# Sixteen float32 attention units by pairs of heads, and weight decoding pinned among VectorE's work

## The chip, the cores and the metric

The kernel runs on one NeuronCore of a Trainium2 chip. TensorE multiplies matrices into PSUM, VectorE (DVE in the rows), ScalarE (ACT) and GpSimd (POOL) work elementwise, SyncE (SP) issues DMAs. The metric is the device time of one execution in microseconds: before, the median of three runs is 740.23 us (740.11 to 740.49).

## The reference

Sliding-window attention with four sink keys, followed by a two-layer feed-forward block whose activation is a clipped square:

```python
scores = scale * q @ k.T                     # B, H, S, D = 4, 8, 768, 64
keep = (pos[None] < n_sink) | ((rel >= 0) & (rel < window))      # 4 sinks, window 128
a = exp(where(keep, scores, -1e9) - max); a = a / (a.sum(-1) + 1e-9)
x = (a @ v) as [3072, 512]
h = x @ w_in                                 # 512 x 2048, stored as float64
g = where(h >= 1, h, where(h <= -1, 0, (h + 1)**2 / 4))
out = g @ w_out                              # 2048 x 512, stored as float64
```

## The kernel before

A *unit* is one head and half of its 768 positions: three tiles of 128 queries, each against the block of 128 keys before, the 4 sinks and its own block. There are 64 units, in eight chunks of eight; chunk 0 is the first half of batch 0, chunk 1 the first half of batch 1, and so on. After a chunk of attention, the feed-forward block runs over its 384 rows, in 16 steps j of `stage1` (x times w_in, 12 products into `h_ps`) and `stage2` (g times w_out, 9 products into `o_ps`).

The first `NATIVE` = 12 units multiply in float32 directly. The other 52 are *split* units: each operand is written as a rounded float32r part and the rest, and each product is made of several fast ones. Feed-forward products are always split (3 for 1).

The weights come as float64 words in 16 loads of 1 MB (two j of w_in, then two j of w_out). `decode` rebuilds each as float32 parts: three integer passes on VectorE over 128 x 1024 elements (L151 to L153), a cast on ScalarE (L154) and a subtraction on VectorE (L155). `weights(n)` issues loads ahead, the first four from SyncE, the others from ScalarE's queue.

What sets the order: TensorE keeps the order of the program. `spread` interleaves two lists of steps by estimated TensorE weights: chunk 0's attention with the first `WFIRST` = 4 decodes, then the feed-forward steps of chunk 0, which carry the other 12 decodes, with the attention of chunk 1, and so on. On the other engines a scheduler places each instruction by its own estimate of when its inputs are there, so a decode may run far ahead of its place in the program.

A native unit before: `scores` (three products L244 over 128 partitions that hold q and k twice, hence the scale -0.0625; a masked scaling with the row's peak L248 on VectorE; the exponential with its sum L251 on ScalarE), the normalising of p (L256 on GpSimd, L257, L269 on ScalarE and L271 on VectorE), `transp` (seven transposes L324, L326 and three ScalarE copies) and `av` (four products L390 that leave 64 rows of x transposed, and a copy L392). `split` (L458, L459) then cuts x for the feed-forward block.

Of the kernel before, what the change touches and what calls it, by code (L numbers as in the profile page):

```python
# [51 lines left out]
def attn_ffn(ctx, tc, qk, vx, vs, par, w_in, w_out, out):  # L52
# [180 lines left out]
    def scores(u, i):  # L233
# [25 lines left out]
        c0 = 0  # L259
        if units.index(u) >= NATIVE:  # L260

            c0 = P
            nc.vector.tensor_tensor(p[:, i0:, KB:260], p[:, i0:, KB:260], p[:, i0:, 0:P], op=ALU.add)
        for i in range(CT):
            lo = KB if t0 + i == 0 else c0
            r = stat[:, CT + i:CT + i + 1]
            eng = NORM[i] if units.index(u) < NATIVE else "v"
            if eng == "a":
                nc.scalar.activation(p[:, i, lo:260], p[:, i, lo:260], AF.Copy, scale=r)  # L269
            else:  # L270
                (nc.gpsimd if eng == "p" else nc.vector).tensor_scalar(p[:, i, lo:260], p[:, i, lo:260], r, None,  # L271
                                                                       op0=ALU.mult)
        if units.index(u) < NATIVE:
            sk = None
        else:
            sk = att.tile([P, CT * NSINK], F32, name="sk")[:, :(CT - i0) * NSINK]
            nc.vector.tensor_copy(sk.rearrange("p (i s) -> p i s", s=NSINK), p[:, i0:, P:KB])
# [371 lines left out]
```

## Time and profile before

| | us |
|---|---|
| median of three runs | 740.23 |
| profiled execution, whole time | 741.25 |
| profiled execution, span from first to last instruction | 739.5 |
| TensorE busy | 703.0 (95%) |
| VectorE busy | 531.0 (72%) |
| ScalarE busy | 509.5 (69%) |
| GpSimd busy | 326.9 (44%) |

The shares are means over stages that differ: until the first feed-forward product TensorE has gaps, and after it nearly none. The profiled execution took 741.25 us, of which 1.75 us lie outside the span; it is 1.02 us longer than the median of the runs.

### The profile page before, as it was taken

How to read it: one execution, taken by the hardware profiler on the slowest of the kernel's cores; microseconds unless marked ns; L12 is line 12 of the kernel's file. 1: busy time of each engine (PE TensorE's matmuls, PEld its weight loads, DVE VectorE, ACT ScalarE, POOL GpSimd, SP SyncE). 2: the span in 40 equal slices, each digit the busy share in tenths (PEclk: the TensorE clock that was granted, in tenths of full speed). 3: DMA queues.
4: the chain of work that ended last, by engine and by line, in shares of the span. 5: the costliest groups of instructions: out<-in, count | busy, mean ns of one | idle time of the engine just before them, and what ended most of it. 6: DMA issues, size and time to landing. Idle time of an engine off the chain costs nothing.

```text
span 739.5 us, 12343 instructions
## 1 busy us (share of the span) xinstructions
PE 703.0 (95%) x3837; PEld 621.8 (84%) x3837; DVE 531.0 (72%) x1360; ACT 509.5 (69%) x1309; POOL 326.9 (44%) x562
## 2 busy tenths in 40 slices
PE   3787899999999999999999999999989999999996
PEld 2444788899999999999889998899979999989995
DVE  7999955757776887877877887878888577742221
ACT  4787676767777877777776876778767776544332
POOL 3111456754554454645565564646556344400000
PEclk9999999999999999999999999999999999999999
DMA  8977331213123433334434433424422220001001
GB/s 295 332 252 253 97 99 44 58 46 95 55 60 132 144 116 114 99 111 124 135 89 123 142 117 96 121 68 161 123 85 67 64 78 28 9 1 44 0 1 47
DMA packets 43236, 76.25 MB, mean 103 GB/s; under 512 B 7324, under 2 KB 27804, under 8 KB 43164
## 3 DMA queue, kind: packets, MB, share of 16 engines
q1 hardware_dynamic: 39900, 62.81, 27.5%
q10 hardware_dynamic: 3264, 12.58, 4.8%
q8 instruction: 32, 0.52, 0.3%
q14 instruction: 40, 0.33, 0.1%
HBM read 69.09 MB, written 6.29 MB: 102 GB/s over the span
## 4 chain that ended last, share of the span: by engine, by line
PE 72%; DVE 11%; ACT 6%; DMA 4%; issue 3%; POOL 2%; SPq 0%; ACTq 0%; POOLq 0%
PE h_ps L428 30%; PE o_ps L447 30%; PE ps_a L390 6%; PE ps_a L244 4%; ACT p L251 2%; PE ps_a L336 2%; DVE p L271 1%; DMA w<-w_in 1%; POOL stat L256 1%; DVE k_s L228 1%; DVE bits L152 1%; DMA again<-w_in 1%; DVE bits L153 1%; DMA r<-qk 1%; DVE g L437 1%
## 5 line engine op out<-in xcount | busy, mean ns | idle before, releaser
L428 PE MATMUL h_ps<-x,wi 128*128 128x384 f32 x1536 | 310.2, 341 | 2.8 <-DVE g L437 1.9
L428 PEld LDWEIGHTS h_ps<-x,wi 128*128 128x128 f32 x1536 | 263.6, 189 | 11.8 <-DVE g L437 2.2
L447 PE MATMUL o_ps<-w,gh 128*128 128x512 f32 x768 | 243.0, 397 | 0.0
L447 PE MATMUL o_ps<-w,gl 128*128 128x512 f32 x384 | 151.0, 393 | 0.0
L447 PEld LDWEIGHTS o_ps<-w,gh 128*128 128x128 f32 x768 | 134.0, 188 | 15.3 <-ACT g L436 0.4
L251 ACT ACTIVATE p<-p,peak 128x260 f32<-128x260 f32 (+1 forms) x192 | 93.9, 489 | 35.6 <-DVE peak L248 34.3
L435 ACT ACTIVATE g<-h_ps,half 128x384 f32<-128x384 f32 x128 | 74.0, 578 | 61.7 <-PE h_ps L428 61.2
L230 POOL TENSOR_TENSOR q_l<-r,q_h 128x384 fp32r<-128x384 f32 x52 | 53.8, 1034 | 137.9 <-ACT q_h L229 120.3
L437 DVE SCALAR_TENSOR_TENSOR g<-g,h_ps 128x384 f32<-128x384 f32 x128 | 70.2, 548 | 60.1 <-ACT g L436 59.2
L438 ACT CAST gh<-g 128x384 fp32r<-128x384 f32 x128 | 65.5, 512 | 52.8 <-DVE g L437 52.0
L248 DVE CUSTOM_DVE_ANT_0 p<-ps_a,m 128x260 f32<-128x260 f32 (+1 forms) x192 | 74.5, 400 | 24.8 <-PE ps_a L244 23.5
L447 PEld LDWEIGHTS o_ps<-w,gl 128*128 128x128 f32 x384 | 72.0, 188 | 17.3
L439 DVE TENSOR_TENSOR gl<-g,gh 128x384 fp32r<-128x384 f32 x112 | 68.2, 609 | 24.4 <-ACT gh L438 23.4
L228 DVE TENSOR_TENSOR k_s<-k_r,k_s 64x524 fp32r<-64x524 f32 (+1 forms) x46 | 48.1, 1047 | 43.6 <-ACT k_s L226 43.5
L244 PE MATMUL ps_a<-k_s,q_h 128*128 128x260 f32 (+1 forms) x228 | 65.9, 332 | 14.2 <-DMA k_s<-qk 7.6
L390 PE MATMUL ps_a<-pt,v_s 128*128 128x256 f32 (+2 forms) x396 | 68.2, 297 | 1.4 <-DVE peak L248 1.1
L436 ACT ACTIVATE g<-g 128x384 f32<-128x384 f32 x128 | 67.0, 524 | 2.6
L390 PEld LDWEIGHTS ps_a<-pt,v_s 128*128 128x128 f32 (+1 forms) x396 | 58.9, 183 | 9.5 <-issue 2.4
L244 PEld LDWEIGHTS ps_a<-k_s,q_h 128*128 128x128 f32 x228 | 43.2, 204 | 27.3 <-issue 8.5
L256 POOL TENSOR_SCALAR stat<-stat 128x3 f32<-128x3 f32 x64 | 32.7, 511 | 72.4 <-ACT p L251 60.6
L348 POOL TENSOR_SCALAR_AFFINE_SELECT pt<-pt 128x384 fp32r<-128x384 f32 (+1 forms) x104 | 53.8, 519 | 24.0 <-DVE pt L341 21.0
L271 DVE TENSOR_SCALAR p<-p,stat 128x132 f32<-128x132 f32 (+1 forms) x168 | 62.9, 424 | 0.2
(108 smaller groups left out, 954.5 us busy)
## 6 DMA issues: line engine op xcount, KB each, us to landing
r<-qk SPq DMA_DIRECT2D x52, 192.0 KB
k_r<-qk SPq DMA_DIRECT2D x32, 262.0 KB
again<-w_in SPq DMA_DIRECT2D x16, 512.0 KB
again<-w_out SPq DMA_DIRECT2D x16, 512.0 KB
w<-w_in ACTq DMA_DIRECT2D x6, 1024.0 KB
w<-w_out ACTq DMA_DIRECT2D x6, 1024.0 KB
out<-o SPq DMA_DIRECT2D x23, 256.0 KB
r<-vx SPq DMA_DIRECT2D x32, 128.0 KB
```

Source lines behind the costliest of these rows:

```text
L244: nc.tensor.matmul(ps[:, lo:260], lhsT=q[:, i * P:(i + 1) * P], rhs=k_s[:, c0:c0 + 260 - lo], start=(j == 0), stop=(j == len(qs) - 1))
L248: nc.vector.tensor_tensor_reduce(out=p[:, i, lo:260], in0=ps[:, lo:260], in1=m, scale=-0.0625 if units.index(u) < NATIVE else -0.125, scal ...
L251: nc.scalar.activation(p[:, i, lo:260], p[:, i, lo:260], AF.Exp, bias=peak_i, scale=-1.0, accum_out=stat[:, i:i + 1])
L271: (nc.gpsimd if eng == "p" else nc.vector).tensor_scalar(p[:, i, lo:260], p[:, i, lo:260], r, None, op0=ALU.mult)
L390: nc.tensor.matmul(z, lhsT=w, rhs=y, start=(n == 0), stop=(n == len(mms) - 1))
L428: nc.tensor.matmul(h_ps[:, :T], lhsT=w_i[j][:, w, ct * P:(ct + 1) * P], rhs=x[:, y, ct], start=(ct == 0 and n == 0), stop=(ct == NCT - 1 a ...
L435: nc.scalar.activation(g, h_ps[:, :T], AF.Relu, bias=half, scale=0.5)
L436: nc.scalar.activation(g, g, AF.Square)
L437: nc.vector.scalar_tensor_tensor(g, g, 1.0, h_ps[:, :T], op0=ALU.min, op1=ALU.max)
L438: nc.scalar.copy(gh, g)
L439: (nc.gpsimd if row0 == GL_POOL else nc.vector).tensor_tensor(gl, g, gh.bitcast(F32), op=ALU.subtract)
L447: nc.tensor.matmul(o_ps[tt], lhsT=gg[:, tt * P:(tt + 1) * P], rhs=w_o[j][:, w], start=(j == 0 and n == 0), stop=(j == NJ - 1 and n == 2))
```

## The change

Units 0 to 15 (chunks 0 and 1) are now native, in pairs of heads. One new input `qkp` holds a pair's two heads in the two halves of the 128 partitions, so each score product contracts over 64 partitions, and a pair needs one load of q and one of k. p is not normalised: it is transposed as it leaves the exponential, and becomes the stationary operand of products with v, to which a column of ones is added; column 65 of the result is the sum, and a VectorE pass divides the three tiles by it (`early_av`). Three transposes per pair (`pair_x`) bring x into the layout that `split` reads. In the tile of the first queries but one, a new mask `m1n` lets the sinks be read from the block before. Chunk 0's scores also use the PSUM tiles of the feed-forward block.

The first instruction of every decode is kept at its place in the program's order on VectorE, and the first four weight loads are issued after a pair's k load. Units 16 to 63 are computed as before; the subtraction of k in units 16 to 19 is on GpSimd (before: 12 to 17).

```diff
-NATIVE = 12
+NATIVE = 16
-KL_POOL = range(12, 18)
+KL_POOL = range(16, 20)
...
+    m1n = const.tile([P, 260], F32, name="m1n")
...
+    nc.vector.tensor_copy(m1n, m2)
+    nc.vector.tensor_tensor(m1n[:, 0:P], m2[:, 0:P], skp, op=ALU.max)
+    nc.gpsimd.memset(m1n[:, P:KB], 0.0)
...
-    def decode(t, w, words):
+    def decode(t, w, words, pin=False):
...
-        nc.vector.tensor_scalar(w, x, 3, 0x3FFFFFFF, op0=ALU.logical_shift_left, op1=ALU.bitwise_and)
+        first = nc.vector.tensor_scalar(w, x, 3, 0x3FFFFFFF, op0=ALU.logical_shift_left, op1=ALU.bitwise_and)
+        if pin:
+            tc.keep_in_program_order(first)
...
-            for k in range(n, min(n + min(AHEAD, NP // 2 - n // 2 - 1) + 1, NP)):
+            for k in range(n, min(n + min(AHEAD if n > 2 else 1, NP // 2 - n // 2 - 1) + 1, NP)):
...
-                    (nc.sync if k < SYNC else nc.scalar).dma_start(raw[k], src(k))
+                    with tc.issue_after(loaded[-1]) if k < SYNC else nullcontext():
+                        (nc.sync if k < SYNC else nc.scalar).dma_start(raw[k], src(k))
...
-            decode(t, dec.tile([P, 2, DM], I32, name="bits"), words)
+            decode(t, dec.tile([P, 2, DM], I32, name=f"bits{n % 2}"), words, pin=True)
...
+    def pair_load(m):
+        b, h, _ = units[2 * m]
+        T = CT * P
+        W = CT * KB - NSINK
+        q_s = att.tile([P, T], F32R, name="q_h").bitcast(F32)
+        k_s = att.tile([P, P + CT * KB], F32R, name="k_s").bitcast(F32)[:, :W]
+        loaded.append(nc.sync.dma_start(k_s, qkp[b, h // 2, :, T:T + W]).ins)
+        nc.sync.dma_start(q_s, qkp[b, h // 2, :, 0:T])
+        st["qk", m] = q_s, k_s
+    def pair_values(m):
+        for a in range(2):
+            b, h, _ = units[2 * m + a]
+            v_s = vq[(2 * m + a) % 4]
+            nc.sync.dma_start(v_s[:, :CT, :D], vx[b, h, :, :CT])
+            nc.sync.dma_start(v_s[:NSINK, CT, :D], vs[b, h, :NSINK])
+    def early_p(u):
+        return (p0[u % 2] if u // 2 % 2 == 0 else pt0[u % 2][:, 5 * P:5 * P + CT * 260]).rearrange(
+            "p (i c) -> p i c", c=260)
+    def pair_scores(m, i):
+        q_s, k_s = st["qk", m]
+        lo, c0 = (KB if i == 0 else 0), max(0, (i - 1) * KB)
+        banks = []
+        for a in range(2):
+            pool, name = ((ps_o, "o_ps"), (ps_o, "o_ps"), (ps_o, "o_ps"), (ps_h, "h_ps"), (ps_h, "h_ps"),
+                          (ps_a, "ps_a"))[2 * i + a] if m <= H // 2 - 1 else (ps_a, "ps_a")
+            ps = pool.tile([P, 512], F32, name=name)
+            r = slice(a * D, a * D + D)
+            nc.tensor.matmul(ps[:, lo:260], lhsT=q_s[r, i * P:(i + 1) * P], rhs=k_s[r, c0:c0 + 260 - lo],
+                             start=True, stop=True)
+            banks.append(ps)
+        for a, ps in enumerate(banks):
+            u = 2 * m + a
+            p = early_p(u)[:, i, lo:260]
+            peak_i = peak[:, u, i:i + 1]
+            nc.vector.tensor_tensor_reduce(out=p, in0=ps[:, lo:260], in1=(m0, m1n, m2)[i], scale=-0.125, scalar=3.0e38,
+                                           op0=ALU.add, op1=ALU.min, accum_out=peak_i)
+            nc.scalar.activation(p, p, AF.Exp, bias=peak_i, scale=-1.0)
+    def early_transp(u, part):
+        p, pt = early_p(u), pt0[u % 2]
+        ps = ps_a.tile([P, 512], F32, name="ps_a")
+        for n, (i, c) in enumerate((((0, KB), (1, 0), (1, KB)), ((2, 0), (2, KB)))[part]):
+            nc.tensor.transpose(ps[:, n * P:(n + 1) * P], p[:, i, c:c + P], ident)
+        if part:
+            nc.tensor.transpose(ps[:NSINK, 2 * P:CT * P], p[:, CT - 1, P:KB], ident)
+            nc.scalar.copy(pt[:, CT * P:5 * P], ps[:, :2 * P])
+            nc.scalar.copy(spn[u % 2][:NSINK], ps[:NSINK, 2 * P:CT * P])
+        else:
+            nc.scalar.copy(pt[:, :CT * P], ps[:, :CT * P])
+    def early_av(u):
+        pt, v_s = pt0[u % 2], vq[u % 4]
+        if u % 2 == 0:
+            st["xq", u // 2] = att.tile([P, CT * P], F32R, name="q_l").bitcast(F32).rearrange(
+                "p (i a d) -> p i a d", a=2, d=D)
+        stat = att.tile([P, 2 * CT], F32, name="stat")
+        ps = ps_a.tile([P, 512], F32, name="ps_a")
+        z = ps[:, :CT * (D + 1)].rearrange("p (i d) -> p i d", d=D + 1)
+        for i, blocks in enumerate((((0, 0),), ((1, 0), (2, 1)), ((3, 1), (4, 2), (None, CT)))):
+            for n, (s0, k) in enumerate(blocks):
+                w = spn[u % 2] if s0 is None else pt[:, s0 * P:(s0 + 1) * P]
+                nc.tensor.matmul(z[:, i], lhsT=w, rhs=v_s[:, k], start=(n == 0), stop=(n == len(blocks) - 1))
+        nc.vector.tensor_scalar(stat[:, 0:CT], z[:, :, D], 1.0e-9, None, op0=ALU.add)
+        nc.vector.reciprocal(stat[:, CT:2 * CT], stat[:, 0:CT])
+        nc.vector.tensor_tensor(st["xq", u // 2][:, :, u % 2], z[:, :, :D],
+                                stat[:, CT:2 * CT].unsqueeze(2).broadcast_to([P, CT, D]), op=ALU.mult)
+    def pair_x(m):
+        xq = st.pop(("xq", m))
+        ps = ps_a.tile([P, 512], F32, name="ps_a")
+        for i in range(CT):
+            nc.tensor.transpose(ps[:, i * P:(i + 1) * P], xq[:, i].rearrange("p a d -> p (a d)"), ident)
+        nc.scalar.copy(xn[:, units[2 * m][1] // 2, :], ps[:, :CT * P])
+    def pair_steps(m):
+        a, b = 2 * m - 2, 2 * m - 1
+        end = m % (H // 2) == 0
+        sc = [(0.45, lambda i=i: pair_scores(m, i)) for i in range(CT)] if m < NATIVE // 2 else [(0.0, lambda: None)] * CT
+        x = [(0.4, lambda: pair_x(m - 2))] if m % (H // 2) != 1 else []
+        steps = [(0.0, lambda: pair_load(m + 1))] if m + 1 < NATIVE // 2 else []
+        if m < NATIVE // 2:
+            steps.append((0.0, lambda: pair_values(m)))
+        if not m:
+            return [(0.0, lambda: pair_load(0))] + steps + sc
+        tp = [(0.45, lambda u=u, i=i: early_transp(u, i)) for u in (a, b) for i in range(2)]
+        pv = [(1.4, lambda u=u: early_av(u)) for u in (a, b)]
+        if end:
+            return (steps + tp[:1] + x + tp[1:3] + pv[:1] + tp[3:] + sc[:1] + pv[1:] + sc[1:]
+                    + [(0.4, lambda: pair_x(m - 1))])
+        return steps + tp[:1] + x + sc[:1] + tp[1:3] + sc[1:2] + pv[:1] + tp[3:] + sc[2:] + pv[1:]
...
-        if 1 in us:
+        if 1 in us and n - 1 >= NATIVE:
...
-    dec = early.enter_context(tc.tile_pool(name="dec", bufs=2))
+    dec = early.enter_context(tc.tile_pool(name="dec", bufs=1))
+    vq = [dec.tile([P, CT + 1, D + 1], F32, name=f"vq{i}") for i in range(4)]
...
+    p0 = [att.tile([P, CT, 260], F32, name="p").rearrange("p i c -> p (i c)") for _ in range(2)]
+    pt0 = [att.tile([P, 2, CT, 2, P], F32R, name="pt").bitcast(F32).rearrange("p a i c q -> p (a i c q)")
+           for _ in range(2)]
...
-        attn = [step for n in range(n0, n1) for step in attn_steps(n)]
+        if c < 2:
+            attn = [step for m in range((0, 5)[c], (5, 9)[c]) for step in pair_steps(m)]
+            if c:
+                attn += [step for n in range(NATIVE, n1) for step in attn_steps(n)]
+        else:
+            attn = [step for n in range(n0, n1) for step in attn_steps(n)]
...
+    qkp = qk[:, :, 0].reshape(B, H // 2, P, QK)
```

The first place is VectorE's work in the middle of chunk 0's attention. `bits<-w` are a decode's integer passes, `w` and `wi` on the left its results, `p,peak<-ps_a` the masked scalings of a unit's scores, `x<-xn` a `split`. Before:

```order
L152 SCALAR_TENSOR_TENSOR bits<-w,bits 128x1024
L257 RECIPROCAL stat<-stat 128x3
L151 TENSOR_SCALAR bits<-w 128x1024
L248 ISA p,peak<-ps_a,m_108 128x128
L248 ISA peak 128x1
L248 ISA p,peak<-ps_a,m_107 128x260
L248 ISA peak 128x1
L153 SCALAR_TENSOR_TENSOR bits<-w,bits 128x1024
L459 TENSOR_TENSOR x<-xn,x 128x384
L271 TENSOR_SCALAR p<-p,stat 128x128
```

The same place now, from the first row of a decode on; `q_l<-ps_a,stat` is the division of a unit's x by its sums:

```order
L150 TENSOR_SCALAR bits_311<-w 128x1024
L153 SCALAR_TENSOR_TENSOR bits_311<-w,bits_311 128x1024
L388 ISA p,peak<-o_ps,m_109 128x128
L388 ISA peak 128x1
L388 ISA p,peak<-o_ps,m_109 128x128
L388 ISA peak 128x1
L508 TENSOR_TENSOR x<-xn,x 128x384
L154 SCALAR_TENSOR_TENSOR bits_311<-w,bits_311 128x1024
L388 ISA p,peak<-o_ps,m1n 128x260
L388 ISA peak 128x1
L388 ISA p,peak<-h_ps,m1n 128x260
```

Before, parts of two decodes stand among the scalings of one unit; now the parts of one decode stand among those of a pair. Up to the last `split` of chunk 0 VectorE's list held 11 whole decodes and one without its last row; it holds 4 whole ones and two rows of a fifth.

The second place is TensorE's work where the feed-forward block begins (`h_ps<-x,wi`). Before:

```order
L390 MATMUL ps_a<-spn_139,vsn_141 64x256
L244 MATMUL ps_a<-k_s,q_h 128x128
L428 MATMUL h_ps<-x,wi_146 128x384 x3
L244 MATMUL ps_a<-k_s,q_h 128x260
L428 MATMUL h_ps<-x,wi_146 128x384 x9
```

Now; `ps_a<-ident,q_l` is `pair_x`, the rows with 65 columns are p times v:

```order
L417 MATMUL ps_a<-vq_168,pt 128x65 x5
L417 MATMUL ps_a<-vq_168,spn_170 128x65
L381 MATMUL ps_a<-k_s,q_h 128x260 x4
L427 MATMUL ps_a<-ident,q_l 128x128 x3
L397 MATMUL ps_a<-ident,p 128x128 x3
L477 MATMUL h_ps<-x,wi_143 128x384 x3
L381 MATMUL ps_a<-k_s,q_h 128x128 x2
```

The block now begins behind the scores of units 8 and 9, the last `pair_x` of chunk 0 and three transposes of unit 8. From the first `h_ps` of chunk 1 on, the same feed-forward steps follow on TensorE as before.

## Rows read from the trace of the kernel before

**Rows 1.** Windows: stretch, its length, busy us (instructions) of each engine, granted clock, DMA share, GB/s.
```profile
0.00:7.20 7.20, 2.39 (x6) 1.60 (x6) 4.57 (x19) 1.28 (x1) 4.54 (x28) 1.00 0.58 182
7.20:69.70 62.50, 45.47 (x185) 26.81 (x184) 59.22 (x129) 46.70 (x129) 8.41 (x12) 0.95 0.84 299
69.70:162.40 92.70, 88.60 (x479) 76.76 (x479) 65.09 (x154) 64.89 (x169) 52.12 (x74) 0.98 0.26 77
162.40:739.50 577.10, 566.56 (x3174) 516.64 (x3172) 402.08 (x1060) 396.62 (x1012) 261.82 (x450) 1.00 0.28 85
```

**Rows 2.** Timeline of TensorE: start, us, line, out<-in, shape, count [idle before <-releaser].
```profile
69.67 0.78 PE L428 MATMUL h_ps<-x,wi 128*128 128x384 f32 x3
73.02 0.62 PE L428 MATMUL h_ps<-x,wi 128*128 128x384 f32 x2 [0.91 <-DVE x L459]
78.52 1.23 PE L428 MATMUL h_ps<-x,wi 128*128 128x384 f32 x3 [1.92 <-DVE g L437]
162.38 0.69 PE L428 MATMUL h_ps<-x,wi 128*128 128x384 f32 x3
```

**Rows 3.** Groups of VectorE's instructions, 0 to 73.1 us: count | busy, mean ns | idle before.
```profile
L152 DVE SCALAR_TENSOR_TENSOR bits<-w,bits 128x1024 int32<-128x1024 int32 x12 | 14.8, 1230 | 0.0
L151 DVE TENSOR_SCALAR bits<-w 128x1024 int32<-128x1024 int32 x13 | 9.0, 695 | 2.6 <-DMA w<-w_in 2.6
L248 DVE CUSTOM_DVE_ANT_0 p<-ps_a,m 128x260 f32<-128x260 f32 x21 | 8.7, 422 | 0.2
L155 DVE TENSOR_TENSOR wi<-bits,wi 128x1024 fp32r<-128x1024 f32 x6 | 7.3, 1223 | 0.0
L155 DVE TENSOR_TENSOR w<-bits,w 128x1024 fp32r<-128x1024 f32 x5 | 6.1, 1221 | 0.0
L248 DVE CUSTOM_DVE_ANT_0 p<-ps_a,m 128x128 f32<-128x128 f32 x11 | 3.1, 279 | 0.0
```

**Rows 4.** Timeline of VectorE: the first scaling, then four instructions of chunk 0's attention.
```profile
7.24 0.28 DVE L248 CUSTOM_DVE_ANT_0 p<-ps_a,m 128x128 f32<-128x128 f32 x1
...
57.32 0.43 DVE L248 CUSTOM_DVE_ANT_0 p<-ps_a,m 128x260 f32<-128x260 f32 x1
...
57.67 0.56 DVE L459 TENSOR_TENSOR x<-xn,x 128x384 fp32r<-128x384 f32 x1
58.14 1.23 DVE L152 SCALAR_TENSOR_TENSOR bits<-w,bits 128x1024 int32<-128x1024 int32 x1
59.27 0.29 DVE L271 TENSOR_SCALAR p<-p,stat 128x128 f32<-128x128 f32 x1
```

**Rows 5.** Timeline of TensorE: a unit's scores twice, then attention among feed-forward products.
```profile
18.25 2.50 PE L244 MATMUL ps_a<-k_s,q_h 128*128 128x128 f32 x6 [2.79 <-DMA k_s<-qk]
50.63 1.37 PE L244 MATMUL ps_a<-k_s,q_h 128*128 128x128 f32 x6
101.81 0.28 PE L244 MATMUL ps_a<-k_s,q_h 128*128 128x260 f32 x1
101.92 0.28 PE L244 MATMUL ps_a<-k_s,q_l 128*128 128x260 f32 x1
102.75 0.27 PE L324 MATMUL ps_a<-ident,p 128*128 128x128 f32 x1
102.86 0.27 PE L326 MATMUL ps_a<-ident,p 128*4 128x128 f32 x1
106.39 1.30 PE L390 MATMUL ps_a<-pt,v_s 128*64 128x128 f32 x6
108.05 0.73 PE L447 MATMUL o_ps<-w,gh 128*128 128x512 f32 x2
```

**Rows 6.** Groups of VectorE's instructions, 69.7 to 162.4 us.
```profile
L152 DVE SCALAR_TENSOR_TENSOR bits<-w,bits 128x1024 int32<-128x1024 int32 x4 | 6.5, 1630 | 0.0
L155 DVE TENSOR_TENSOR w<-bits,w 128x1024 fp32r<-128x1024 f32 x3 | 3.7, 1221 | 0.7 <-ACT w L154 0.7
L151 DVE TENSOR_SCALAR bits<-w 128x1024 int32<-128x1024 int32 x4 | 3.1, 774 | 2.3 <-DMA w<-w_out 2.3
```

More of the change, by code (lines that the diff above doesn't have):

```diff
@@ L1 @@
-from contextlib import ExitStack
+from contextlib import ExitStack, nullcontext
 import concourse.bass as bass
@@ L51, in attn_ffn @@
 @with_exitstack
[L52 removed]
+def attn_ffn(ctx, tc, qk, qkp, vx, vs, par, w_in, w_out, out):
     nc = tc.nc
@@ L110, in attn_ffn @@
     nc.vector.tensor_tensor(m1[:, 0:P], m1[:, 0:P], skp, op=ALU.mult)
-    for m in (m0, m1, m2):
+    for m in (m0, m1, m1n, m2):
         nc.vector.tensor_scalar(m, m, -1.0, -NEG, op0=ALU.add, op1=ALU.mult)
@@ L258, in scores @@
         i0 = int(t0 == 0)
[L259 to L263, printed above, removed]
+        nc.vector.tensor_tensor(p[:, i0:, KB:260], p[:, i0:, KB:260], p[:, i0:, 0:P], op=ALU.add)
         for i in range(CT):
[L265 to L277, printed above, removed]
+            lo = KB if t0 + i == 0 else P
+            nc.vector.tensor_scalar(p[:, i, lo:260], p[:, i, lo:260], stat[:, CT + i:CT + i + 1], None, op0=ALU.mult)
+        sk = att.tile([P, CT * NSINK], F32, name="sk")[:, :(CT - i0) * NSINK]
+        nc.vector.tensor_copy(sk.rearrange("p (i s) -> p i s", s=NSINK), p[:, i0:, P:KB])
         st["p", u] = (p, sk)
@@ L311, in transp @@
         r = ns * NSINK
[L312 removed]
+        spt = st["sp", u] = sp[units.index(u) % 2]
         ps = ps_a.tile([P, 512], F32, name="ps_a")
         pk = ps[:r, T:512]
[L315 to L318 removed]
+        pt = st["pt", u] = att.tile([P, 2, CT, 2, P], F32R, name="pt")
         pth, ptl = pt[:, 0], pt[:, 1]
[L320 to L334 removed]
         for i in range(CT):
@@ L370, in av @@
             terms.append((0, 1))
-        native = units.index(u) < NATIVE
         mms = []
@@ L378, in av @@
                 w, c = v_s[:, (s0 + 1) // 2 - i0], s0 // 2
[L379 to L380 removed]
+                rhs = [pt[:, j].rearrange("p i c q -> p (i c q)")[:, s0 * P:s1 * P] for j in range(2)]
+                if n == 0:
                     rhs = [pt[:, :, CT - 1, 1]]
[L382 to L387 removed]
+            mms += [(w.rearrange("p a d -> p (a d)"), y, c * P) for y in rhs]
         for n, (w, y, c) in enumerate(mms):
[L389 removed]
+            z = ps[:, c:c + (2 * P if len(y.shape) == 3 else y.shape[-1])]
             nc.tensor.matmul(z, lhsT=w, rhs=y, start=(n == 0), stop=(n == len(mms) - 1))
[L391 to L393 removed]
         nc.scalar.copy(x, ps[D - r0:P - r0, :T])
@@ L410, in attn_steps @@
             steps.append((0.0, lambda: load(us[-1])))
-        if 1 in us:
+        if 1 in us and n - 1 >= NATIVE:
             steps.append((0.0, lambda: values(us[1])))
-        qk = [(0.43 if n < NATIVE else 0.22, lambda i=i: scores(us[0], i)) for i in range(CT) if 0 in us]
-        tp = [(0.43, lambda i=i: transp(us[1], i)) for i in range(2 if n - 1 < NATIVE else 1) if 1 in us]
-        pv = [(1.4 if n - 2 < NATIVE else 1.0, lambda: av(us[2]))] if 2 in us else []
-        steps += qk + tp + pv
+        steps += [(0.22, lambda i=i: scores(us[0], i)) for i in range(CT) if 0 in us]
+        steps += [(0.43, lambda: transp(us[1]))] if 1 in us and n - 1 >= NATIVE else []
+        steps += [(1.0, lambda: av(us[2]))] if 2 in us and n - 2 >= NATIVE else []
         if n in CHECK:
```

70 lines of the change are left out of this document (12 added, 58 removed).

## The prediction

> **What bounds the kernel now.** I read the busy time by windows first, cut where the work changes, then TensorE's timeline at the cuts, then VectorE's groups and timeline ahead of the first cut. TensorE starts its first `h_ps` product at 69.67 us, and the first of chunk 1 at 162.38 [rows 2]. Between 7.2 and 69.7 us VectorE is busy 59.22 of 62.50 us, TensorE only 45.47 and ScalarE 46.70. Behind that TensorE is busy 88.60 of 92.70 us, then 566.56 of 577.10 [rows 1]. So the opening is VectorE's and the rest is TensorE's. TensorE's list is unchanged from the first `h_ps` of chunk 1 on; those 577.1 us stay, and the change is worth whatever it moves the 162.38.
>
> What fills VectorE in the opening is decoding: 12 of the 16 decodes, though the program places 4 there [rows 3]. From one start to the next an instruction takes 0.08 to 0.10 us less than its duration: 0.35 of 0.43, 0.47 of 0.56, 1.13 of 1.23 [rows 4]. So a scaling L248 costs 0.20 (128 wide) or 0.35 (260), a `split` 0.47, and a decode 0.61 + 3 x 1.13 = 4.0. To test the method I add up the list of before to its last `split`: masks until the first scaling, 7.2; scalings 11 x 0.20 + 21 x 0.35 = 9.5; 11 decodes 44.0 and 2.9 of a twelfth; small normalising work, nine L271 at 0.20 and ten reciprocals at 0.09, 2.7; four splits 1.9; the wait for the first weights 2.6 [rows 3, 4]. That is 70.8, and the product that the last `split` released starts at 73.02 [rows 2]: VectorE's list, with 3% of gaps, set the opening.
>
> **The change part by part.** *Opening, VectorE.* To its last `split` the list now holds 4 decodes (16.0) and 1.7 of a fifth; scalings 12 x 0.20 + 20 x 0.35 = 9.4; splits 1.9; masks 8.2 (three operations more for `m1n`, each between L248's two steps); the wait for the first weights 2.6, unless a pair's loads, half the bytes of before, bring it earlier; and eight divisions by the sums. That division is not in the trace. Two operations on three columns are small, 0.08 each by the overlap above; the one on 192 columns lies between a 128-wide L248 (0.20) and a 384-wide split (0.47). I take 0.27, by the nearer row, so 0.43 a unit and 3.4 in all (2.9 to 5.0). Sum 43.2 us, 30 less than 73.02. This is a floor: before, decodes filled VectorE's waits; pinned, they can't, and attention shows its own chain of scores, scaling, exponential, transposes, copy, products, division, transposes, split.
>
> *Opening, TensorE.* A unit's scores are one float32 product of 128 and two of 260 columns. Their six records took 2.50 us at 18.25 and 1.37 at 50.63 [rows 5]: the clock's two levels, 1.2 and 2.4 GHz, though the granted clock averages 0.95 there [rows 1]. The slow ones stood behind a wait of 2.79. At the higher level they cost 1.37 less the tail of one record: 0.27 long, 0.11 to the next start [rows 5], so 0.16; I take 1.1 with small change. A transpose costs 0.11. The products with v are now six of 65 columns a unit. Bounds: one transpose each (0.11, as wide a stationary operand) or two (0.22, since a float32 product is two records); I take the middle, 0.16, so 1.0 a unit against 108.05 - 106.39 = 1.66 before [rows 5]. A pair costs 2 x (1.1 + 6 x 0.11 + 1.0) + 3 x 0.11 = 5.9 us at 2.4 GHz, 11.7 at 1.2. VectorE's share of a pair, one decode included, is 1.8 + 4.0 + 0.9 + 0.5 = 7.2. ScalarE was busy 75% [rows 1] and loses normalising passes and seven casts of weights; it stays below VectorE.
>
> Two engines at 6 and 7 us that wait for each other in fixed order don't overlap fully; I take 9 us a pair, a quarter above VectorE's share. (Nothing in the trace gives this quarter; its bounds are 7.2 and the 13 of both in turn.) The first pair's scores start near 5 us and take 4.4 at 1.2 GHz; the second block takes 11 at that clock; three of 9 follow: 5 + 4.4 + 11 + 27 = 47.4, say 48 us for the first `h_ps`. The opening gets 69.7 - 48 = 21.7 shorter, between 26 (VectorE's floor) and 12 (the first rival).
>
> *Chunk 0 of the feed-forward block.* Its products are the same before and now, so only attention's part of TensorE's list changes; I count it in the two orders. Before: native scores 2.0; 21 transposes 2.3; four units' native values at 1.66, 6.6; of the split units seven scores, five transposes and four values at 0.11 a record [rows 5], 9.2; together 20.1. Now: native scores, 6 products of 128 columns at 0.22 and 12 of 260 at 0.43, 6.5; 41 transposes and 12 in `pair_x`, 5.8; 48 products with v 7.7 (5.3 to 10.6); split units 2.2; together 22.2. That is 2.1 more: native units cost more than the split ones they replace.
>
> VectorE carries 11.5 decodes here instead of about 4.6: 46 us; with the 15 operations L437 at 0.47, 6.8 of scalings, 3.4 of divisions and 4 for units 16 to 18 it has 67. Beside GpSimd's work L152 took 1.63 us on average instead of 1.23 [rows 3, 6]; on 11 decodes that adds 4.4. 72 of 94 us is 76%, against 70% before [rows 1]. TensorE will now and then meet a PSUM tile that VectorE hasn't read; the wait of 1.92 for L437 [rows 2] was such a case. I add 1.3 us. A decode stands two steps j ahead of the products that read it, about 8 us of cover; if that goes, see the third rival.
>
> Sum: -21.7 + 2.1 + 1.3 = -18.3. The profiled execution's 741.25 becomes 722.9; the median of the runs is 1.0 lower: **721.9 us**.
>
> Two rules of the Trainium skill pull apart here. No product of before contracts over 64 partitions, so no row shows what a pair of them costs; I took two full products. "TensorE: Matmul & The Clock Gate", in its part on packing small matmuls, says that products in distinct row groups run at once; by it the scores in this stretch cost 3.3 us less, 718.6. "TensorEngine Tiling (Array Packing)", Key Properties, speaks against the change: switching the tiling mode drains the engine. With the tail of a record, 0.16 us [rows 5], into and out of nine pairs, that is 2.9 more, 724.8.
>
> **The rivals.** *The opening runs at the low clock* (0.15). TensorE was busy 73% of the opening, and early waits left it at 1.2 GHz [rows 1, 5]; a pair gives it no more work now. Four blocks of 11.7 and the start put the first `h_ps` at 5 + 4.4 + 47 = 56, with some waits 58: -11.7 + 3.4, so 731.9. Against it: the unit at 50.63 ran at 2.4, in an opening with as many gaps.
>
> *VectorE alone sets the opening* (0.12). If its list stays full the first `h_ps` comes at 43; with 0.11 per product with v, chunk 0 takes 2.4 less than taken above: 26.7 + 2.4 - 3.4 gives 714.5, and with pairs of scores at once and no added waits 708. Against it: the pinning.
>
> *Decoding binds chunk 0* (0.15). Each decode's last row waits for ScalarE's cast, which stands behind exponentials and casts of g. If that costs 2.2 us a decode, twice the 1.13 of a pass as large, 12 of them add 26 to VectorE's 72 and waits for TensorE the rest: 103 us instead of 92.7. The time is 741.25 - 21.7 + 10.3 - 1.0 = 728.9. For it: VectorE can't put other decodes there any more. Against it: that wait came to 0.7 us on three decodes [rows 6].
>
> *Late weights, slower than before* (0.05). The loads leave ScalarE's queue behind pinned casts. If each of the 12 decodes waits for its 1 MB, the chunk takes 12 periods of load, decode and cast. The gain is gone when a period exceeds (92.7 + 21.7) / 12 = 9.5 us; at 11 it is 132, and the time 757.8. Against it: such waits came to 2.6 us in the opening and 2.3 in chunk 0 [rows 3, 6], and chunk 0 moved 77 GB/s where the opening moved 299 [rows 1].
>
> **How the numbers follow.** The forecast has 0.53, its own range 714 to 728. I leave out two tenths in all: the lowest end of the second rival, the fourth, and the first and third together. That gives 708 to 737. 0.2%, 1.5 us, is what a measurement can tell from no change; only the first and third rival together (740) land there, 0.03. Faster 0.92, same 0.03, slower 0.05.
>
> **What would show it.** The first `h_ps` near 48 us, with VectorE below 95% busy until then; decode steps spread over chunk 0; the first `h_ps` of chunk 1 near 144, and 577 us behind it. If a pair's score products start together, the 718.6 was right. The prediction is wrong if the first `h_ps` comes after 58 or chunk 0 takes over 103 us.

## The result, and the profile after

The changed kernel takes 734.88 us (median of 4 runs, 732.49 to 748.24) against 740.17: a ratio of 0.992 [0.990, 0.994]. Ratios here leave out executions more than 1.5% above the fastest of their kernel. The forecast was 721.9. Executions of the changed kernel differ among themselves by up to 17 us, with the level of TensorE's clock in the opening, so two profiles of the same code are shown: the first of 748.24 us, the second (from the first experiment) of 734.92.

By windows, cut at the first `h_ps` product and at the first of chunk 1 (columns as in [rows 1]), the profile of 748.24 us:

```profile
7.20:61.94 54.74, 50.38 (x209) 38.11 (x208) 35.01 (x113) 27.01 (x66) 1.40 (x5) 1.00 0.63 207
61.94:167.81 105.87, 97.58 (x541) 84.48 (x539) 86.86 (x158) 62.50 (x140) 35.70 (x33) 0.94 0.33 108
167.81:746.50 578.69, 566.49 (x3174) 516.68 (x3172) 403.75 (x1060) 397.52 (x1012) 262.41 (x450) 1.00 0.29 85
```

and the profile of 734.92 us:

```profile
7.20:50.26 43.06, 36.67 (x207) 27.47 (x208) 34.19 (x113) 26.24 (x65) 1.40 (x5) 0.96 0.71 237
50.26:154.48 104.22, 95.00 (x542) 81.87 (x540) 87.54 (x159) 62.97 (x141) 35.34 (x33) 0.95 0.35 118
154.48:733.10 578.62, 566.92 (x3174) 516.50 (x3172) 403.03 (x1060) 397.84 (x1012) 261.21 (x450) 1.00 0.28 85
```

Against [rows 1] the opening ends 8 us earlier in the one and 19 in the other; chunk 0 of the feed-forward block is 13.2 and 11.5 us longer in both; the rest is 1.6 and 1.5 longer. VectorE now has slack in the opening (34 of 43 us busy) and carries 87 us in chunk 0, where it had 65.

What parts the two openings shows on TensorE's timeline of the products with v (start, us, line, names, shape, count). In the profile of 748.24 us:

```profile
26.43 2.39 PE L417 MATMUL ps_a<-vq,pt 128*128 128x65 f32 x10
```

and in that of 734.92 us, with the scores of a pair ahead of them:

```profile
25.26 0.80 PE L381 MATMUL o_ps<-k_s,q_h 64*128 64x260 f32 x1
25.26 0.80 PE L381 MATMUL h_ps<-k_s,q_h 64*128 64x260 f32 x1
25.85 0.63 PE L381 MATMUL o_ps<-k_s,q_h 64*128 64x260 f32 x1
25.86 0.63 PE L381 MATMUL h_ps<-k_s,q_h 64*128 64x260 f32 x1
26.42 1.33 PE L417 MATMUL ps_a<-vq,pt 128*128 128x65 f32 x10
...
28.03 0.27 PE L399 MATMUL ps_a<-ident,pt 128*4 128x128 f32 x1
28.23 0.48 PE L381 MATMUL h_ps<-k_s,q_h 64*128 64x260 f32 x1
28.24 0.48 PE L381 MATMUL ps_a<-k_s,q_h 64*128 64x260 f32 x1
28.55 0.38 PE L381 MATMUL h_ps<-k_s,q_h 64*128 64x260 f32 x1
28.56 0.38 PE L381 MATMUL ps_a<-k_s,q_h 64*128 64x260 f32 x1
```

From 10 to 26.4 us the two stand at the same instruction within 0.02 us. Then one runs the ten products in 1.33 us (2.4 GHz), the other in 2.39 (1.2 GHz), and stays there for every unit up to 54.7 us. The pair's two products do start 0.01 us apart.

Where chunk 0 loses its time, in the profile of 734.92 us: TensorE's waits from 50 to 155 us (us in all, times, longest), then its timeline at the longest of them, then VectorE's.

```profile
PE ps_a L295 <- DVE p L259: 6.3, 3, 4.5
PE ps_a L417 <- ACT pt L400: 2.1, 1, 2.1
PE ps_a L240 <- DVE peak L244: 0.5, 1, 0.5
PE h_ps L477 <- DVE g L486: 0.3, 1, 0.3
```

```profile
132.46 0.28 PE L240 MATMUL ps_a<-k_s,q_l 128*128 128x260 f32 x1
132.58 0.62 PE L496 MATMUL o_ps<-w,gh 128*128 128x512 f32 x2
133.04 0.40 PE L496 MATMUL o_ps<-w,gl 128*128 128x512 f32 x1
137.93 0.47 PE L295 MATMUL ps_a<-ident,p 128*128 128x128 f32 x1 [4.49 <-DVE p L259]
138.55 0.45 PE L295 MATMUL ps_a<-ident,p 128*128 128x128 f32 x1 [0.15 <-DVE p L259]
140.70 0.45 PE L295 MATMUL ps_a<-ident,p 128*128 128x128 f32 x1 [1.70 <-DVE p L259]
141.08 0.38 PE L296 MATMUL ps_a<-ident,sk 128*8 128x128 f32 x1
141.11 4.19 PE L477 MATMUL h_ps<-x,wi 128*128 128x384 f32 x12
```

```profile
132.11 1.82 DVE L153 SCALAR_TENSOR_TENSOR bits<-w,bits 128x1024 int32<-128x1024 int32 x1
...
134.41 1.21 DVE L154 SCALAR_TENSOR_TENSOR bits<-w,bits 128x1024 int32<-128x1024 int32 x1
...
135.89 1.10 DVE L256 TENSOR_TENSOR p<-p 128x256 f32<-128x256 f32 x1
136.92 0.54 DVE L486 SCALAR_TENSOR_TENSOR g<-g,h_ps 128x384 f32<-128x384 f32 x1
137.38 0.16 DVE L253 RECIPROCAL stat<-stat 128x3 f32<-128x3 f32 x1
137.58 0.82 DVE L259 TENSOR_SCALAR p<-p,stat 128x128 f32<-128x128 f32 x2
138.33 2.02 DVE L156 TENSOR_TENSOR w<-bits,w 128x1024 fp32r<-128x1024 f32 x1
140.28 0.28 DVE L259 TENSOR_SCALAR p<-p,stat 128x132 f32<-128x132 f32 x1
```

Unit 16 is now the first split unit. Its last scores ran at 129.09, and TensorE's list has its transposes (L295) due by 133.4: three feed-forward products behind the last scores of unit 17, and some 4 us behind unit 16's own. VectorE, in that time, stands in a decode: passes of 1.82 and 1.21 us ahead of the normalisation (L256, L259) and one of 2.02 ahead of its third part. Behind the wait twelve `h_ps` products take 4.19 us, 0.35 each, twice the 0.17 of those at 2.4 GHz, and the granted clock from 138 to 146 us is 0.51: the clock fell after the wait as well.

The 2.1 us at L417 (122.72) have a like root: on ScalarE's timeline the copy that these products wait for (L400) stands behind a cast of weights that had waited 3.6 us for VectorE's pass L154.

### The profile page after: what moved, and what is told of

The parts are those of the page before. It is cut to its first block, busy times and chain, and to the rows that moved or that the text cites. A ratio compares the mean times of both kernels' runs of the same rounds, so it can differ in the third digit from the quotient of the medians.

```text
span 746.5 us, 12285 instructions
## 1 busy us (share of the span) xinstructions
PE 716.8 (96%) x3929; PEld 641.0 (86%) x3929; DVE 530.2 (71%) x1345; ACT 488.3 (65%) x1217; POOL 304.5 (41%) x519
## 4 chain that ended last, share of the span: by engine, by line
PE 69%; DVE 15%; ACT 6%; DMA 4%; POOL 3%; issue 2%; POOLq 0%; ACTq 0%
PE h_ps L477 26%; PE o_ps L496 26%; PE ps_a L417 4%; PE ps_a L342 3%; PE ps_a L240 3%; DMA again<-w_out 2%; DVE p L259 2%; PE ps_a L295 1%; DVE k_s L224 1%; DMA r<-qk 1%; PE ps_a L397 1%; ACT p L247 1%; DVE g L486 1%; DVE gl L488 1%; PE ps_a L381 1%
## 5 line engine op out<-in xcount | busy, mean ns | idle before, releaser
L226 POOL TENSOR_TENSOR q_l<-r,q_h 128x384 fp32r<-128x384 f32 x48 | 50.2, 1047 | 137.4 <-ACT q_h L225 109.6
L247 ACT ACTIVATE p<-p,peak 128x260 f32<-128x260 f32 (+1 forms) x144 | 71.4, 496 | 15.5 <-DVE peak L244 14.6
L244 DVE CUSTOM_DVE_ANT_0 p<-ps_a,m 128x260 f32<-128x260 f32 (+1 forms) x144 | 57.3, 409 | 21.6 <-PE ps_a L240 20.5
L306 POOL TENSOR_SCALAR_AFFINE_SELECT pt<-pt 128x384 fp32r<-128x384 f32 (+1 forms) x96 | 51.2, 534 | 24.1 <-DVE pt L299 20.9
L304 POOL TENSOR_SCALAR_AFFINE_SELECT pt<-pt 128x384 fp32r<-128x384 f32 (+1 forms) x96 | 51.8, 540 | 10.1 <-ACT pt L298 5.9
L488 POOL TENSOR_TENSOR gl<-g,gh 128x384 fp32r<-128x384 f32 x16 | 21.2, 1324 | 82.7 <-ACT gh L487 82.7
L259 DVE TENSOR_SCALAR p<-p,stat 128x132 f32<-128x132 f32 (+1 forms) x144 | 53.1, 422 | 0.1
L342 PEld LDWEIGHTS ps_a<-pt,v_s 128*128 128x128 f32 x304 | 46.4, 188 | 2.2
L342 PE MATMUL ps_a<-pt,v_s 128*128 128x256 f32 (+1 forms) x304 | 46.7, 274 | 0.0
L240 PE MATMUL ps_a<-k_s,q_h 128*128 128x260 f32 (+1 forms) x144 | 40.2, 280 | 4.7 <-DVE sk L301 3.9
```

What stands on the lines that cost most here:

```text
L240: nc.tensor.matmul(ps[:, lo:260], lhsT=q[:, i * P:(i + 1) * P], rhs=k_s[:, c0:c0 + 260 - lo], start=(j == 0), stop=(j == len(qs) - 1))
L244: nc.vector.tensor_tensor_reduce(out=p[:, i, lo:260], in0=ps[:, lo:260], in1=m, scale=-0.125, scalar=3.0e38, op0=ALU.add, op1=ALU.min, acc ...
L247: nc.scalar.activation(p[:, i, lo:260], p[:, i, lo:260], AF.Exp, bias=peak_i, scale=-1.0, accum_out=stat[:, i:i + 1])
L259: nc.vector.tensor_scalar(p[:, i, lo:260], p[:, i, lo:260], stat[:, CT + i:CT + i + 1], None, op0=ALU.mult)
L342: nc.tensor.matmul(z, lhsT=w, rhs=y, start=(n == 0), stop=(n == len(mms) - 1))
L488: (nc.gpsimd if row0 == GL_POOL else nc.vector).tensor_tensor(gl, g, gh.bitcast(F32), op=ALU.subtract)
```

## The experiments

Two theories for chunk 0 stood against each other: A, VectorE is short of time with 12 pinned decodes; C, the order leaves one place without cover, that is, without other products between asking for a result and reading it. (B, in some expectations: TensorE's own list is longer.) For the opening: the clock theory, TensorE's level sets it, against the chain theory, waits in fixed order set it and the clock follows.

**The kernel again, unedited** (`e1_again`).

> The changed kernel once more, unedited, since its one profile is 12 us longer than its other runs. Clock theory (the opening is TensorE's work at 1.2 GHz): median 733 to 736; first h_ps at 60 to 63 us with a transpose still at 0.21 us from start to start in nearly all of the opening; the 12 us more of the first profile lie in chunk 0's feed-forward stretch, so the first h_ps of chunk 1 comes near 155 instead of 168. Chain theory (waits in fixed order set the opening, the clock only follows): the opening differs from the first profile, first h_ps before 55.

745.27 us (734.92 to 749.67, 12 runs), before 739.99: 1.003 [1.000, 1.006]. In this series the change gains nothing; the same code gave 734.9 in one and 745.3 in the other, so that a gain over the kernel before is not shown. The clock theory's median was missed, and the first `h_ps` of the profiled execution, 50.26, is what the chain theory named; yet the two openings part at one instruction, in the duration of its products and with no wait ahead of it. In the profiles of versions with these score products and no fillers, the ten products with v first run at 2.4 GHz at 26.4 (here), 26.7 (`e8`), 39.8 (`e5`) and 53.3 us (`e14`), and in that of 748.24 us nowhere in the opening.

**Fillers: four products of 384 columns on zeros ahead of each of the first eight units' products with v** (`e2_filler`).

```
+        if u < H:
+            for _ in range(4):
+                nc.tensor.matmul(ps[:, :CT * P], lhsT=sp[0][:, :P], rhs=sp[0], start=True, stop=True)
```

> Changed kernel with four float32r products of 384 columns on zeros ahead of every unit's products with v in chunk 0 (overwritten, 32 products more). Clock theory: the fillers lift TensorE to 2.4 GHz after the first pairs; transposes at 0.11, first h_ps at 45 to 52 although there is 5 to 10 us more work; time 720 to 730. Chain theory: the fillers only add their own time (0.16 to 0.32 us each, 5 to 10 us): first h_ps at 66 to 72, time 740 to 746.

732.43 (731.18 to 733.05): 0.989 [0.987, 0.991]. The first `h_ps` stands at 47.70, and the first ten products take 1.22:

```profile
15.03 1.22 PE L420 MATMUL ps_a<-vq,pt 128*128 128x65 f32 x10
```

TensorE had more work and the opening got shorter, as the clock theory had it; its time was missed by 2.4 us, since chunk 0 stayed at 104.9. The fillers raise the clock early in most executions, not in all: in the later profiles with fillers the first ten products took 2.23 three times (`e6`, `e12`, `e15`).

**Score products over all 128 partitions** (`e3_k128`).

```
-            r = slice(a * D, a * D + D)
+            r = slice(0, P)
```

> Changed kernel whose score products contract over all 128 partitions, so that each adds up both heads' scores (the attention of units 0 to 15 is not the reference's). This undoes the products over 64 partitions alone. If these small products are what leaves the clock low: the clock rises, first h_ps at 45 to 55, time 720 to 730. If the 65-column products do it: the clock stays low, and the scores, no longer two at once, cost 24 x 0.6 us more in the opening's low clock; first h_ps at 70 to 76, time 740 to 750.

726.21 (723.86 to 726.86): 0.980 [0.978, 0.982]. The first `h_ps` at 42.60, and the first ten products with v already in 1.30:

```profile
12.68 1.30 PE L417 MATMUL ps_a<-vq,pt 128*128 128x65 f32 x10
...
14.26 0.27 PE L399 MATMUL ps_a<-ident,p 128*4 128x128 f32 x1
14.37 0.60 PE L381 MATMUL h_ps<-k_s,q_h 128*128 128x260 f32 x2
14.81 0.60 PE L381 MATMUL ps_a<-k_s,q_h 128*128 128x260 f32 x2
```

Chunk 0 is 104.8. So the low level came with the score products over 64 partitions; whether by the half of the partitions or by two of them running at once, this edit does not part. The 65-column products are not the cause: they are still there. At the upper level the opening comes down to VectorE's list, forecast at 43.2: VectorE is busy 33.40 of the 35.40 us up to 42.60.

**Pinning alone, in the kernel before** (`e4_pin_only`): `keep_in_program_order` for a decode's first instruction and nothing else.

> The kernel before with only the pinning of each decode's first instruction. Clock theory: with native units as before (scores over 128 partitions, values in 256 columns) the clock rises and VectorE is no longer full, so the opening shrinks to 45 to 55 us and the time falls to 715 to 728, below the changed kernel. Rival (pinned decodes bind chunk 0's feed-forward stretch): the opening shrinks, but chunk 0 grows by as much, time 735 to 742.

749.87 (748.68 to 750.81): 1.013 [1.010, 1.015], 1.3% longer. The windows:

```profile
7.20:57.29 50.09, 39.72 (x184) 24.50 (x184) 32.31 (x101) 39.20 (x122) 4.28 (x12) 1.00 0.69 242
57.29:171.57 114.28, 98.95 (x478) 83.24 (x478) 105.28 (x182) 71.26 (x176) 68.23 (x72) 0.90 0.38 121
```

The opening ends 12.4 us earlier, and chunk 0 is 21.6 longer, with VectorE busy 92% of it. What pinning takes out of the opening comes back with interest. That is the rival's direction; both expectations put the time too low.

**The change without pinning** (`e7_no_pin`): `decode(..., pin=True)` becomes `decode(...)`.

> The changed kernel without the pinning of the decodes' first instruction. Theory A: the decodes drift into the opening as before (about 12 there), the first h_ps comes at 60 to 72 and chunk 0 takes 92 to 96 us, so 730 to 742: the pinning is worth within 8 us of nothing, since it moves decodes from one bound to another. Rival (the pinning brings the gain, as the forecast had it): 745 to 755, the opening filled with decodes and chunk 0 no shorter.

761.53 (755.94 to 765.53): 1.025 [1.018, 1.032]. Both expectations were too low. 13 decodes drift into the opening; the first `h_ps` comes at 85.1:

```profile
7.20:85.10 77.90, 49.41 (x209) 36.67 (x208) 67.55 (x149) 35.80 (x75) 1.09 (x5) 0.68 0.68 229
```

VectorE's list sets this opening: it is busy 67.55 of the 77.90 us and waits 9.0 of the rest for weights (6.4 us more than before). So the rest of the change needs the pinning: without it attention waits for VectorE, and TensorE for both. Chunk 0, expected at 92 to 96, took 100.6, its first 20 us at a granted clock of 0.66 to 0.75. It holds three decodes only, VectorE is busy 43 us of it, and the wait ahead of unit 16's transposes is 0.9 us.

**More decodes in the opening** (`e5_first8`; `e6_filler_first8` with the fillers), `WFIRST = 4` to `8`; **and fewer** (`e10_filler_first2`), `2`.

> The changed kernel with 8 instead of 4 decodes placed in the opening. Theory A (chunk 0 is bound by VectorE, which carries 12 pinned decodes there): four decodes of 4 to 5 us leave chunk 0, which shrinks from about 105 to 90 to 95 us; the opening has room on VectorE and grows by 4 to 10, so 726 to 738 (and up to 745 where the opening stays at 1.2 GHz). Rival B (chunk 0 is long for TensorE's own longer list, not for the decodes): chunk 0 stays near 105, the opening grows by up to 16, so 745 to 760.

> The four filler products of 384 columns before the products with v of each unit of chunk 0 (the second experiment, 732.4) and 8 decodes in the opening together. Theory A: the opening keeps the upper clock and VectorE's slack there takes the four decodes; first h_ps at 52 to 60, chunk 0 near 92, 720 to 728. Rival B: chunk 0 stays above 100, so 737 to 748.

> The second experiment's kernel with 2 instead of 4 decodes in the opening. From 4 to 8 the first h_ps came 18.3 us later with fillers, 4.6 a decode, and chunk 0 got 6.2 shorter, 1.5 a decode. If that goes on downwards: first h_ps near 38.5, chunk 0 near 108, 726. If VectorE is at its limit in chunk 0 (Theory A), each of the two decodes costs its full 4 to 5 us there: chunk 0 near 114, 731 to 735.

741.35 (1.002 [0.999, 1.004]), 744.88 (1.003 [1.000, 1.006]) and 736.12 (0.995 [0.991, 0.999]). With fillers, 2, 4 and 8 decodes put the first `h_ps` at 48.80, 47.70 and 66.03, and chunk 0 takes 107.0, 104.9 and 98.7 us. Two decodes less bring the opening nothing (38.5 was expected), so four stand there for free; four more cost 18.3, part of it a low clock in the first pairs (the ten products take 2.23), and give back 6.2. Theory A expected 90 to 95 for chunk 0 with 8 decodes there: it missed, since the wait ahead of L295 was still there, 3.5 us in `e5_first8`. Rival B missed too, in chunk 0: it had it above 100 with fillers. With 2 decodes there theory A expected 114 for chunk 0, which took 107.0.

**`gl` of chunk 0 on VectorE instead of GpSimd** (`e8_gl_vector`; `e11_filler_glv` with fillers), `GL_POOL = 0` to `-1`.

> The changed kernel with the subtraction for gl of chunk 0 on VectorE instead of GpSimd. If the operations of VectorE are drawn out mainly because GpSimd works beside them, VectorE takes 16 subtractions of about 0.5 us more and loses more than that in dilation: chunk 0 gets 3 to 8 us shorter, 727 to 735. If VectorE is simply full by its count of instructions, chunk 0 gets 5 to 10 us longer: 740 to 755.

> The second experiment's kernel with gl of chunk 0 on VectorE instead of GpSimd. The run without fillers gave chunk 0 of 100.6 with its first part at the low clock. If VectorE's operations are drawn out by GpSimd's: chunk 0 at 98 to 101, 726 to 729, the passes of the decodes nearer 1.2 us than 1.9. If that gain was only another opening: 732 to 735.

733.08 (0.983 [0.976, 0.990]) and 728.55 (0.984 [0.980, 0.987]). VectorE got sixteen operations more and chunk 0 shorter, 100.6 and 99.4. VectorE's groups (count | busy, mean ns | idle before), first in chunk 0 of the changed kernel at 734.92 us, then from 45 to 150 us of `e11`:

```profile
L153 DVE SCALAR_TENSOR_TENSOR bits<-w,bits 128x1024 int32<-128x1024 int32 x12 | 18.6, 1553 | 0.2
L154 DVE SCALAR_TENSOR_TENSOR bits<-w,bits 128x1024 int32<-128x1024 int32 x12 | 16.9, 1405 | 0.2
L150 DVE TENSOR_SCALAR bits<-w 128x1024 int32<-128x1024 int32 x12 | 9.8, 815 | 0.9 <-DMA w<-w_out 0.9
L156 DVE TENSOR_TENSOR w<-bits,w 128x1024 fp32r<-128x1024 f32 x6 | 9.0, 1494 | 1.4 <-ACT w L155 1.4
...
L156 DVE TENSOR_TENSOR wi<-bits,wi 128x1024 fp32r<-128x1024 f32 x6 | 8.1, 1357 | 2.0 <-ACT wi L155 2.0
```

```profile
L154 DVE SCALAR_TENSOR_TENSOR bits<-w,bits 128x1024 int32<-128x1024 int32 x12 | 14.7, 1221 | 0.1
L153 DVE SCALAR_TENSOR_TENSOR bits<-w,bits 128x1024 int32<-128x1024 int32 x12 | 14.6, 1219 | 0.1
L491 DVE TENSOR_TENSOR gl<-g,gh 128x384 fp32r<-128x384 f32 x16 | 9.6, 597 | 1.2 <-ACT gh L490 1.2
```

The passes over two operands fall from 1.55 and 1.41 to 1.22 us once GpSimd does less beside them (13.5 busy us in chunk 0 instead of 35.3). The wait ahead of unit 16's transposes is still there, 5.2 and 5.3 us; gone are the 2.1 at L417 and the second wait at L295, 1.7.

**An empty step ahead of unit 16's transposes** (`e9_filler_gap` with fillers, `e14_gap_only` without, `e12_filler_gap_first2` with 2 decodes in the opening).

```
+        steps += [(3.0, lambda: None)] if n == NATIVE + 1 else []
         steps += [(0.43, lambda: transp(us[1]))] if 1 in us and n - 1 >= NATIVE else []
```

> The second experiment's kernel (fillers, 732.4) with an empty step of weight 3 ahead of the transposes of unit 16, so that some 6 us more of the feed-forward products stand between the scores of unit 17 and those transposes. Theory C (the end of chunk 0 stalls because the order gives unit 16's scaling almost no cover: 1.4 us of products between its last scores and its transposes): the waits of 4.6, 0.6 and 0.9 us there go, and with them some of the low clock behind; chunk 0 shrinks from 104.9 to 96 to 99 us, 724 to 727. Theory A (VectorE is full with decodes, the stall only shows where the list is tightest): the wait reappears at another product, chunk 0 stays above 102, 730 to 734.

> The changed kernel with the empty step alone, no fillers. The opening is left as it is, so its clock may rise early or late (first h_ps at 48 to 62). If the tight place is a cause of its own, chunk 0 takes 96 to 99 us instead of 104 to 106: 727 to 741, some 6 below the changed kernel (745 when last measured beside before). If the empty step worked only with the fillers: 734 to 748.

> Fillers, the empty step ahead of unit 16's transposes and 2 decodes in the opening together. If the gains of the two add up: 718 to 722. Theory A: VectorE is short of time whatever the order, 730 to 736.

726.59 (726.02 to 727.82), 0.982 [0.979, 0.985]; 734.65 (0.993 [0.989, 0.996]); 736.33 (0.996 [0.993, 0.999]). The step adds no work; it moves TensorE's list. Chunk 0 falls to 97.4 and, without fillers, 97.3, as theory C said; of the waits there the longest left is 2.0. Chunk 0 of `e9`:

```profile
48.76:146.15 97.39, 93.53 (x535) 80.61 (x535) 85.56 (x156) 61.24 (x136) 35.44 (x32) 0.98 0.36 119
```

VectorE is nearly as busy as in the changed kernel (87.54). `e14`'s first `h_ps` came at 58.57, at the low level; its time lies in both of its expected ranges and decides nothing. With 2 decodes in the opening nothing adds up: in the profiled execution, 744.59 us, chunk 0 takes 110.3, and a cast of weights (`wi L155`) holds TensorE 6.3 us. VectorE began that decode only at 143.68, when TensorE was already waiting for it, so theory A holds at that end.

**Both edits of chunk 0** (`e13_filler_gap_glv`), **and half of each decode left out there** (`e15_filler_short_decode`, fillers, tight place kept).

```
-        nc.vector.scalar_tensor_tensor(w, x, -0x40000000, w, op0=ALU.bitwise_and, op1=ALU.bitwise_or)
-        nc.vector.scalar_tensor_tensor(w, low, 29, w, op0=ALU.logical_shift_right, op1=ALU.bitwise_or)
+        if all_passes:   # n < WFIRST; the same two lines, indented
+            ...
```

> Fillers, the empty step ahead of unit 16's transposes, and gl of chunk 0 on VectorE, together. With fillers the empty step alone took chunk 0 from 104.9 to 97.4 us, gl alone to 99.4, with the wait of 5.3 us ahead of the transposes still there. If the two causes are separate (VectorE's operations drawn out beside GpSimd's, and the tight place), chunk 0 takes 94 to 96 and the time is 722 to 725. If both relieve the same wait, it stays at 726 to 728.

> The second experiment's kernel (fillers) with the two middle passes left out of the 12 decodes that stand in chunk 0, so that these weights are not put together from both words. VectorE has 24 passes of 1.2 to 1.9 us less, 29 to 46 us; the order on TensorE stays. If VectorE's time is what makes chunk 0 long: 104.9 falls to 93 to 96, 720 to 724, and the wait ahead of unit 16's transposes nearly goes. If the order alone is the cause: the wait of 4.6 stays, chunk 0 above 100, 727 or more.

726.7 (0.984 [0.981, 0.987]) and 725.19 (0.979 [0.976, 0.981]). Chunk 0 of `e13`, then of `e15`:

```profile
49.96:145.20 95.24, 91.97 (x536) 79.29 (x535) 85.09 (x172) 60.72 (x136) 16.61 (x17) 1.00 0.37 121
```

```profile
51.26:146.68 95.42, 93.27 (x541) 81.19 (x540) 52.99 (x135) 62.82 (x141) 30.48 (x33) 0.98 0.37 122
```

`e13`'s chunk 0 lies in the range given for separate causes, its time in the other's: its first `h_ps` came 1.2 us later than `e9`'s, and the totals are alike within their spread. The gains of the two edits, 7.5 and 5.5 us, don't add up (9.7 together); TensorE is busy 91.97 of the 95.24 us, so that little was left to gain. In `e15` the tight place is kept, and the wait falls from 4.6 (in `e2_filler`) to 1.9 us, on TensorE's timeline:

```profile
133.27 0.79 PE L296 MATMUL ps_a<-ident,p 128*128 128x128 f32 x3 [1.87 <-DVE p L260]
```

(The new lines in `decode` shift L295 to L296.) So neither theory holds alone: the stall needs VectorE late by its decodes, and a place with little cover. Taking away either one gives 95 to 97 us. `e9_filler_gap` and `e13_filler_gap_glv`, 726.6 and 726.7, are the fastest versions here that compute the whole reference, faster than both kernels.

## Why the prediction was right or wrong

The forecast's sum was 48 + 96.1 + 577.1 = 721.2 us of span. The profile of 734.92 us has 50.26 + 104.22 + 578.62 = 733.1: 2.3, 8.1 and 1.5 more. That of 748.24 us has 61.94 + 105.87 + 578.69 = 746.5: 13.9, 9.8 and 1.6 more.

*Opening.* At the upper level the sum came near: 48 forecast, 50.26 with the clock up from 26.4 us on, 47.70 with fillers, though these carry products of their own. In part this is luck. From one pair to the next it took 8.0 us at 2.4 GHz (`e3`, 19.06 to 27.05) and 12.4 and 13.5 at 1.2 (748.24 us, from 10.62 to 23.06 and 36.52), where I took 9 and 11.7; and at 734.92 us the clock rose 6 us later than the sum has it, with a granted clock of 0.66 once more from 40 to 45 us. The choice of the level failed: the first rival (0.15), priced at 58, is what the 748.24 us execution did, 61.94. I had argued from the unit at 50.63 [rows 5], whose products contract over 128 partitions; `e3` shows that these raise the clock where those over 64, in pairs, leave it to chance.

*VectorE alone* (0.12, 43) was a floor: only `e3` came to it, 42.60. The lower end of this rival adds up to 709.9 (714.5 - 3.3 - 1.3), not 708, and the first and third rival together to 738.9, not 740; no chance hangs on either.

*TensorE in chunk 0* was right: 92.7 + 2.1 = 94.8 forecast, 95.2 and 95.4 with most of the stalls gone. Two prices in it were off and cancelled in part: the products with v took 1.28 us a unit (`e2`, 15.03 to 16.31), the upper bound, not 1.0, and the scores in pairs less than two full products.

*The step that failed* in both executions is "72 of 94 us is 76%" and the 1.3 us added behind it: in their place stand 104.2 - 94.8 = 9.4 us. TensorE waited 9.2 us in chunk 0 (4.1 before, which the 94.8 holds) and was busy 95.0, 3.0 more than in `e13`, where the granted clock stayed at 1.00. Two things were off. The size: 12 decodes took 18.6 + 16.9 + 9.8 + 9.0 + 8.1 = 62.4 us of VectorE by their durations, some 58 from start to start (48 operations, 0.09 less each), where I counted 46 + 4.4 = 50.4, and 87.5 of 104.2 us is 84%. I drew out one pass (L152, now L153) beside GpSimd; L150, L154 and L156 are drawn out too. And the inference: a mean share does not show the place where the list is tightest. I gave the decode "8 us of cover" ahead of the products that read it, and didn't ask what stands behind a decode on VectorE: unit 16's normalisation, with 4 us of cover. The order of the program has it: the split units now begin afresh at the end of chunk 0, with the scores of units 16 and 17 close ahead of the transposes of 16.

*Decoding binds chunk 0* (0.15) had the right size, 103 against 104.2, by the wrong price: the wait for ScalarE's cast came to 1.4 + 2.0 us on twelve decodes, not 26. First and third rival together, given 0.03 and 740 us, are nearest to what was measured, 734.9 and 745.3.

*Late weights* didn't come: the wait for `w` in chunk 0 is 0.9 us. It lies right ahead of the tight place (130.56 us), but does not make the stall: in `e2` it is 0.23 there, and the stall 4.6.

*The pinning* as the ground against a full VectorE list was right: without it the list fills again (`e7`).

*Scores in pairs.* The Trainium skill ("TensorE: Matmul & The Clock Gate", its part on packing small matmuls) says that distinct row groups run at once. By the rows they start together, but a pair of 260-column products takes 0.64 us (28.23 to 28.55, twice) at 2.4 GHz where two over 128 partitions take 0.88 in `e3`: a quarter saved, not half. So the sign that I named for the 718.6 came, and the 718.6 counted too much. It was no gain either, given what these products do to the clock. The switch to them, priced at 0.16 us, shows as 0.09: from the last transpose to the first score product 0.20 us (28.03 to 28.23), where `e3` has 0.11 (14.26 to 14.37). It comes three times a pair; the switch back no row here parts from other things.

*The rest*, 1.5 us more behind chunk 0, is not explained by any run here.

## What to carry to other kernels

When work is moved from one stretch to another, the mean share of the engine that receives it is not enough for a price: look in the new order for the place where a result is read soonest after it is asked for, and at what stands ahead of that result on the engine. An empty step at that place was worth nearly as much as taking half of the moved work away (7.5 and 9.5 us of chunk 0). A change that swaps TensorE's products for narrower ones is to be priced at both levels of the clock, and a spread between runs of one kernel is a reason to look at that first.
